# A written-out instruction order laid out anew, with GpSimd and SBUF-only VectorE work taking turns in the plan, and 150 warm-up matmuls of 256 columns in place of 50 of 512

## The chip, the cores and the metric

The kernel runs on one core of a Trainium2 chip. The metric is the device time of one execution in microseconds (us). Besides the 16 DMA engines the core has TensorE (PE; its weight loads are shown as PEld), VectorE (DVE), ScalarE (ACT), GpSimd (POOL) and SyncE (SP), which issues every DMA of this kernel. Each engine runs its own instructions strictly in the order in which the program lists them.

## The reference

Two stages. First a causal attention with a decay, for 8 batches, 8 heads, 576 positions and a head width of 64:

```python
scores = scale * q @ k.T
decay = cum[:, :, :, None] - cum[:, :, None, :]      # cum = cumsum(log(clip(f)))
scores = where(causal, -1e9, scores + decay); attn = softmax(scores)
attn_out = attn @ v
```

The heads' outputs side by side are `x` (8 x 576 x 512). The second stage is a mixture of four experts. Each expert is a causal attention of its own on `x` (`wq[e]`, `wk[e]`, `wv[e]` of 512 x 64), followed by `wo[e]`. A gate `x @ w_gate` picks two of the four experts for each position, and their outputs are added with softmax weights.

## The kernel before, in words

The work is cut into 48 units. A unit is a pair of heads of the first stage (named `a`, batch, pair: `a0_0` to `a7_3`) or a pair of experts of the second (`m0_0` to `m7_1`). Each unit goes through the same steps, each of them a Python generator that emits one or a few instructions between two `yield`s:

- `prep_attn` (lines 395 to 418) loads q and k as `xin`; ScalarE writes the rounded high parts into `kq` and `ka`, and VectorE subtracts them from the input to get the low parts (line 415, 64 x 1152). Two or three copies inside SBUF are DMAs. `prep_moe` (525) makes q and k of an expert pair by 96 matmuls `pp` (line 541) from `xh` and `xl`. `moe_front` (428) makes the values and the gate: matmuls `pv` (line 444), then a row of small VectorE operations.
- `max_pass` (563) computes scores without the decay's low part with matmuls (line 570) into two PSUM buffers `psm`; VectorE takes masked row maxima from them (lines 576, 591, 623, 630). PE turns the maxima (line 635), ScalarE negates them (638), and two small DMAs write them as a row of `kq` (issued at line 393).
- `scores` (660) computes the scores again, transposed, maxima included (lines 669 and 670, two PSUM buffers `pss`). ScalarE takes exp (686 to 725) into `P`, GpSimd zeroes what is above the diagonal (656, 689, 727) and adds the parts of `P` for the row sums into `R` (733 to 739).
- `attend` (745) multiplies by the values (line 758). For two units together `row_sums` (788) and `apply_rows` (839) sum, invert and scale (VectorE lines 811 to 829, 849, 876), and for experts `project_out` (880, matmuls at line 892) writes the output.

Every operation with two numbers has its line in the profile. VectorE operations whose operands all lie in SBUF are those of lines 415, 876, 814 to 829, 630 and most of those of the gate (470 to 502). GpSimd's masks and sums (656, 689, 727 to 739) lie in SBUF too.

Nothing but the string `ORDER` decides in which order the generators advance. Each two characters of it name one of 293 tasks (a step of a unit, or one of five tasks for constants, weights and warm-up), and each time a task is named, its generator runs to its next `yield`. The emitted instructions are then tied together in that order on every engine, SP included. `SLOTS` says for each buffer name which of its copies (two, three or six) the next tile takes. `4w` is `keep_warm` (line 214): matmuls of zeros by zeros into one PSUM bank that nothing reads. `4y`, `4x`, `4z` and `4A` are constants, the decay's rows, their spreading and the weights; `00`, `02`, `03`, `04` are `prep_attn`, `max_pass`, `scores` and `attend` of unit `a0_0`, `05` and `07` `prep_attn` and `max_pass` of `a0_1`.

The loop at line 951:

```python
    for x, y in zip(digits[::2], digits[1::2]):
        i = DIGITS.index(x) * len(DIGITS) + DIGITS.index(y)
        if i not in started:
            started[i] = iter(tasks[i]())
        next(started[i], None)
```

Of the kernel before, what the change touches and what calls it, by code (L numbers as in the profile page):

```python
# [32 lines left out]
0j0j0j080j0f0f08080o0o080f0j0f0j0f080f0j04030o0f0j0o0t0j080j0j0j0j0f0j090j08090f0q0q0q0j0f0f0f0f0f0f0f0q0f0q0q0q
0q0q0o0o0f0j0a0f0j0t090k0f0f0f0f0q0f0v0a0a0a0f0k0a0f0q0d0k0k0A0t0q0q0a0k090k0q0k0k0f0q0g0A0k0k0t0a0t0k0k0k0k0k0t
0a0t0i0q0q0v0q0q0k0v0v0v0k0k0k0a0F0k0k0v0v0q0q0k0q0k0k0v0v0k0g0f0q0k0f0k0k0p0g0q0b0b0q0A0b0b0b0q0b0v0v0v0l0v0q4w
0r0r0r0r0v0b0v0k0r4A4A0A0A0v0v0r0r0k0b0v0f0v0v0k0C0r0v0v0v0b0b0r0r0r0b0r0r0t0C0v0u0C0v0v0r0r0C0r0r0r0r0C0l0A0m0m
0r0r0r0b0r0r0m0C0w0F0w0w0l0m0m0F0b0m0M0C0C0m0m0m0s0v0A0n0B0n0w0w0w0w0w0C0n0n0C0C0C0C0C0H0n0w0n0M0w0w0w0w0n0n0n4A
# [48 lines left out]
2X2X2X30233030322O3131313131312T31313130312T2T2V2T2T2X2T2T2O2X2T31312X2X31352X2O3135311k352O31323525323532323232
# [36 lines left out]
434v4v4v4v4v4v4v  # L123
# [5 lines left out]
xin 01010101011010101001010101101010  # L129
# [16 lines left out]
NWARM = 50  # L146
# [4 lines left out]
def tile_decay_attention_moe(ctx: ExitStack, tc, qk, v, f, w_gate, wq, wk, wv, wo, out):  # L151
    nc = tc.nc
# [850 lines left out]
```

## Time and profile before

| | |
|---|---|
| time, median of 3 runs | 710.05 us (709.86 to 710.18) |
| the profiled execution's own time | 709.44 us |
| its span, first to last instruction | 707.7 us |
| mean granted TensorE clock | 0.990 |
| PE busy | 677.6 us, 96% of the span |
| VectorE, ScalarE, GpSimd busy | 582.2, 447.2, 444.9 us |
| bytes read from and written to HBM | 32.91 MB, 10.35 MB |

The profile shows one execution. A busy PE is not a PE at its best pace, since matmuls are pipelined and the profile models their ends: one matmul of 260 columns is shown with some 285 ns, while twelve in a row take about 1.45 us. The granted clock is told as a share of 2.4 GHz: 1.00 is 2.4 GHz and 0.50 is 1.2 GHz.

### The profile page before, as it was taken

How to read it: one execution, taken by the hardware profiler on the slowest of the kernel's cores; microseconds unless marked ns; L12 is line 12 of the kernel's file. 1: busy time of each engine (PE TensorE's matmuls, PEld its weight loads, DVE VectorE, ACT ScalarE, POOL GpSimd, SP SyncE). 2: the span in 40 equal slices, each digit the busy share in tenths (PEclk: the TensorE clock that was granted, in tenths of full speed). 3: DMA queues.
4: the chain of work that ended last, by engine and by line, in shares of the span. 5: the costliest groups of instructions: out<-in, count | busy, mean ns of one | idle time of the engine just before them, and what ended most of it. 6: DMA issues, size and time to landing. Idle time of an engine off the chain costs nothing.

```text
span 707.7 us, 15337 instructions
## 1 busy us (share of the span) xinstructions
PE 677.6 (96%) x5370; PEld 556.1 (79%) x5370; DVE 582.2 (82%) x1664; ACT 447.2 (63%) x961; POOL 444.9 (63%) x760
## 2 busy tenths in 40 slices
PE   8798999889999999999999999999999999999997
PEld 3675788668887898778887788788987788879874
DVE  6879988988899788979889888887889978775752
ACT  5676756566567756676586665667665755755544
POOL 7497486576676684676557653846945665653470
PEclk9699999999999999999999999999999999999999
DMA  5665432343173325442335233253333342222203
GB/s 169 171 161 158 107 105 68 88 115 81 36 189 119 88 57 161 112 142 66 87 82 175 74 118 97 59 140 113 83 97 101 107 136 55 51 79 53 50 16 119
DMA packets 31230, 72.23 MB, mean 102 GB/s; under 512 B 4137, under 2 KB 4617, under 8 KB 31153
## 3 DMA queue, kind: packets, MB, share of 16 engines
q1 hardware_dynamic: 31153, 71.25, 36.8%
q8 instruction: 42, 0.69, 0.4%
q14 instruction: 35, 0.29, 0.1%
HBM read 32.91 MB, written 10.35 MB: 61 GB/s over the span
## 4 chain that ended last, share of the span: by engine, by line
PE 71%; DVE 20%; ACT 3%; issue 3%; DMA 1%; POOL 0%; DVEq 0%; ACTq 0%
PE pp_m L541 12%; PE pv L444 7%; PE m_a L570 7%; PE s_a L669 6%; PE s_a L670 6%; PE ob_a L758 6%; PE po L892 5%; DVE ka_a L415 4%; PE ob_m L758 3%; DVE junk_a L576 3%; PE m_m L570 3%; PE s_m L669 2%; PE s_m L670 2%; PE oa_a L758 2%; PE warm L217 2%
## 5 line engine op out<-in xcount | busy, mean ns | idle before, releaser
L656 POOL TENSOR_SCALAR_AFFINE_SELECT P_a<-P_a 128x128 f32<-128x128 f32 x128 | 47.0, 372 | 104.5 <-ACT P_a L704 59.2
L669 PE MATMUL s_a<-ka_a 128*128 128x320 f32 (+4 forms) x384 | 108.4, 306 | 0.2 <-ACT pl L725 0.2
L570 PE MATMUL m_a<-kq 128*128 128x320 f32 (+4 forms) x384 | 95.0, 319 | 11.5 <-DVE mxs_a L576 8.3
L670 PE MATMUL s_a<-kq 128*128 128x320 f32 (+4 forms) x384 | 104.3, 298 | 1.1 <-DMA kq<-ms_a 1.1
L576 DVE CUSTOM_DVE_ANT_0 junk_a<-m_a,mask 128x448 bf16<-128x448 f32 (+2 forms) x192 | 91.7, 485 | 15.9 <-PE m_a L570 12.4
L570 PEld LDWEIGHTS m_a<-kq 128*128 128x128 f32 (+1 forms) x384 | 63.9, 185 | 25.9 <-DVE mxs_a L576 13.9
L669 PEld LDWEIGHTS s_a<-ka_a 128*128 128x128 f32 (+1 forms) x384 | 70.6, 184 | 6.8 <-issue 1.9
L549 ACT ACTIVATE kq<-pp_m 64x288 fp32r<-64x288 f32 x128 | 51.8, 405 | 37.7 <-PE pp_m L541 36.1
L733 POOL TENSOR_TENSOR R_a<-P_a 128x448 f32<-128x448 f32 x64 | 75.6, 1181 | 0.0
L554 DVE TENSOR_TENSOR ka_m<-pp_m,kq 64x288 fp32r<-64x288 f32 x128 | 58.2, 455 | 19.0 <-ACT kq L549 14.9
L670 PEld LDWEIGHTS s_a<-kq 128*128 128x128 f32 (+1 forms) x384 | 70.0, 184 | 2.6 <-DMA kq<-ms_a 1.7
L758 PE MATMUL ob_a<-P_a,va 128*64 128x320 f32 (+1 forms) x512 | 67.6, 406 | 0.0
L735 POOL TENSOR_TENSOR R_a<-R_a,P_a 128x320 f32<-128x320 f32 x64 | 61.0, 954 | 3.8
L686 ACT ACTIVATE P_a<-s_a 128x512 f32<-128x512 f32 x64 | 37.0, 595 | 29.0 <-PE s_a L670 28.5
L669 PE MATMUL s_m<-ka_m 128*128 128x192 f32 (+2 forms) x192 | 52.8, 300 | 2.0 <-ACT P_m L686 2.0
L758 PEld LDWEIGHTS ob_a<-P_a,va 128*64 128x64 f32 x512 | 35.8, 137 | 24.0
L670 PE MATMUL s_m<-kq 128*128 128x192 f32 (+2 forms) x192 | 51.3, 295 | 0.2 <-DMA kq<-ms_m 0.2
L415 DVE TENSOR_TENSOR ka_a<-xin_a,kq 64x1152 fp32r<-64x1152 f32 x32 | 48.7, 1521 | 1.1 <-ACT kq L403 0.3
L689 POOL TENSOR_SCALAR_AFFINE_SELECT P_a<-P_a 128x256 f32<-128x256 f32 x64 | 32.8, 518 | 26.0 <-ACT P_a L686 25.9
L576 DVE CUSTOM_DVE_ANT_0 junk_m<-m_m,mask 128x192 bf16<-128x192 f32 (+2 forms) x96 | 45.8, 485 | 3.2 <-PE m_m L570 2.2
L704 ACT ACTIVATE P_a<-s_a 128x448 f32<-128x448 f32 x64 | 34.1, 544 | 22.7 <-PE s_a L670 21.9
L656 POOL TENSOR_SCALAR_AFFINE_SELECT P_m<-P_m 128x128 f32<-128x128 f32 x64 | 20.3, 319 | 44.3 <-ACT P_m L704 26.7
(191 smaller groups left out, 2142.7 us busy)
## 6 DMA issues: line engine op xcount, KB each, us to landing
xin_a<-in_qk_dram SPq DMA_DIRECT2D x32, 576.0 KB
va<-in_v_dram SPq DMA_DIRECT2D x32, 320.0 KB
ka_a<-kq SPq DMA_DIRECT2D x32, 288.0 KB
ka_m<-kq SPq DMA_DIRECT2D x32, 288.0 KB
kq<-ka_a SPq DMA_DIRECT2D x30, 288.0 KB
out_dram<-outb SPq DMA_DIRECT2D x32, 256.0 KB
kq<-ex SPq DMA_DIRECT2D x47, 27.0 KB
kq<-ms_a SPq DMA_DIRECT2D x64, 2.5 KB
```

The lines of the kernel that those rows point to most:

```text
L415: nc.vector.tensor_tensor(lo, x[at], hi.bitcast(F32), ALU.subtract)
L541: nc.tensor.matmul(pp[:, :HS], w[:, c, es], x[c][:, gs], start=(n == 0), stop=(n == 3 * KC - 1))
L549: nc.scalar.activation(hv[h], src[h], AF.Copy)
L554: nc.vector.tensor_tensor(lo[:, h, gs], src[h], hv[h].bitcast(F32), ALU.subtract)
L570: nc.tensor.matmul(dst, qB[0:K, h, i0 : i0 + dst.shape[0]], kB[0:K, h, j0:j1], start=True, stop=True)
L576: nc.vector.tensor_tensor_reduce(jk[:, :n], src, mask[:, MW - n :], 1.0, init, ALU.add, ALU.max, acc)
L656: return nc.gpsimd.affine_select(pv, pv, [[1, 128]], ALU.is_ge, 0.0, base=0, channel_multiplier=-1)
L669: nc.tensor.matmul(dst, kaf[:, c : c + m], qA[:, h, i0:i1], start=True, stop=False)
L670: nc.tensor.matmul(dst, kqf[0:K, c + h * S : c + h * S + m], qB[0:K, h, i0:i1], start=False, stop=True)
L733: g.tensor_tensor(r[:, h, 128:S], q[:, 320:768], q[:, 768:1216], ALU.add)
L735: g.tensor_tensor(r[:, h, 256:S], r[:, h, 256:S], q[:, 1216:1536], ALU.add)
L758: mm = nc.tensor.matmul(dst[64 * h : 64 * h + 64, c0 : c0 + rhs.shape[-1]], vs[h][0:kp, blk], rhs, start=first, stop=last,)
```

## The change

`ORDER` is another list of the same steps. The generators are the same, and each of them runs through the same steps in its own sequence; only how they are interleaved differs. In the plan from which the new list was written, a VectorE operation on SBUF operands alone and a GpSimd operation never run at the same time. `SLOTS` differs in which copy a tile takes in ten of its rows (`P`, `xin`, `xh`, `mxs`, `psm`, `pss`, `ol`, `psx`, `xl`, `outb`, some of them in a few places only). `keep_warm` issues 150 matmuls of 256 columns, not 50 of 512.

Read step by step, the two lists begin so. Before, 43 warm matmuls stand ahead of the first matmul of `max_pass` of `a0_0`, and the other 7 right behind its first two. In the new list 94 stand ahead of it, and 56 stand in groups of 1 to 24 between the matmuls of the first three units, the last two of them just ahead of the second block of scores of `a0_1`. On VectorE, before, the two subtractions of `prep_attn` of `a0_1` stand behind the second and behind the last operation of `max_pass` of `a0_0`; in the new list both stand behind the last one. On GpSimd the small memset of `mxs` (line 566) with which `max_pass` of `a0_2` begins stands behind the first three masks of `a0_0` before, and ahead of the weights' last two parts and of all these masks in the new list. The last steps, from `attend` of `m7_1` on, have the same matmuls behind them in both.

```diff
 ORDER = """
-4y4y4y4y4y4y4y4y4y4y4y4y4y4w4w4x4x4x4x4x4w4w4w4w4w4w4w4w4w4w4w4w4w4w4w4w4w4w4w4w4w4w4w4w4w4w4y004y4A0000004x4w4w
-4w05054w4w4w4w4w4w4w4w4w4w05054w4w00004z024z4z0000024w4w4w4A4A4A4A4w4w4A4w4w4A4A024A024A050205020202020202024A0c
...
+4w4w4w4w4w4w4w4w4w4w4w4w4w4w4w4w4w4w4w4w4w4w4w4w4w4w4w4w4w4w4w4w4w4w4w4w4w4w4w4w4w4w4w4w4w4w4w4w4w4w4w4w4w4w4w4w
+4w4w4w4w4w4w4w4w4w4w4w4w4w4w4w4w4w4w4w4w4w4w4w4w4w4w4y4y4y4y4y4y4y4y4y4y4y4y4y4y4x4x4x4x4x4x4y000000004A050505
+00024A4A074w4w4w4w4w4w4w4w4w4w4w004w020500004z02024w4w020202024w4w4w4w4w4w020202024w4w4z020202020202024z4A024A4A
...
 SLOTS = """
-P 01010101101010101010101010101010101010101010101010
+P 01010101010101010101010101010101011010101010101010
...
-NWARM = 50
+NWARM = 150
 NACT = 2
...
     def keep_warm():
         wps = ptile(ps_o, "o", "warm")
         for _ in range(NWARM):
-            nc.tensor.matmul(wps, wz[:, 0:128], wz, start=True, stop=True)
+            nc.tensor.matmul(wps[:, :256], wz[:, 0:128], wz[:, :256], start=True, stop=True)
             yield
```

## Rows read from the trace of the kernel before

**Rows 1.** Busy time by stage: each engine's us and instructions, then clock, DMA share, GB/s.

```profile
12.50:36.00 23.50, 17.67 (x76) 13.40 (x73) 18.98 (x56) 15.13 (x24) 11.94 (x23) 0.71 0.73 188
36.00:100.00 64.00, 59.36 (x457) 45.51 (x456) 56.71 (x141) 42.32 (x87) 49.73 (x78) 1.00 0.48 133
100.00:680.00 580.00, 566.78 (x4645) 478.09 (x4645) 485.89 (x1427) 372.75 (x823) 365.34 (x626) 1.00 0.35 95
```

**Rows 2.** The same view, the stretches of 2 us around the lower clock.

```profile
16.00:18.00 2.00, 0.89 (x3) 0.48 (x3) 1.52 (x6) 0.47 (x1) 1.28 (x1) 1.00 0.82 269
...
20.00:22.00 2.00, 1.51 (x5) 1.09 (x5) 1.97 (x3) 0.27 (x1) 1.93 (x4) 0.50 0.76 219
...
32.00:34.00 2.00, 1.95 (x12) 1.74 (x11) 1.49 (x7) 1.31 (x4) 0.59 (x2) 0.73 0.52 159
```

**Rows 3.** PE in order of time: start, us, instructions, [idle before <- releaser].

```profile
1.26 11.67 PE L217 MATMUL warm<-wz 128*128 128x512 bf16 x43 [1.26 <-DVE wz L212]
12.58 0.61 PE L570 MATMUL m_a<-kq 128*128 128x192 f32 x2
13.03 1.69 PE L217 MATMUL warm<-wz 128*128 128x512 bf16 x7
...
16.73 0.59 PE L570 MATMUL m_a<-kq 128*128 128x256 f32 x2 [1.65 <-DVE mxs_a L576]
```

**Rows 4.** What VectorE waited for from 12.5 to 36 us: total us, times, longest.

```profile
DVE junk_a L576 <- PE m_a L570: 3.6, 5, 1.3
DVE junk_a L576 <- POOL mxs_a L566: 0.9, 1, 0.9
```

**Rows 5.** VectorE in order of time: its first maximum, and that of the third unit.

```profile
13.34 0.36 DVE L576 CUSTOM_DVE_ANT_0 junk_a<-m_a,mask 128x192 bf16<-128x192 f32 x1 [1.27 <-PE m_a L570]
...
32.38 0.36 DVE L576 CUSTOM_DVE_ANT_0 junk_a<-m_a,mask 128x192 bf16<-128x192 f32 x1 [0.93 <-POOL mxs_a L566]
```

**Rows 6.** GpSimd in order of time, around the memset that released it.

```profile
31.36 0.29 POOL L656 TENSOR_SCALAR_AFFINE_SELECT P_a<-P_a 128x128 f32<-128x128 f32 x1 [1.12 <-ACT P_a L704]
31.61 0.10 POOL L566 MEMSET mxs_a<- 64x2 f32 x1
```

**Rows 7.** The chain that ended last: start, us, what; runs without a wait, and a transfer.

```profile
75.57 2.79 DMA kq<-ms_a
...
163.14 1.45 PE pv L444 x12
...
301.68 1.40 PE po L892 x6
```

**Rows 8.** VectorE groups by shape: busy us, mean ns of one | idle before.

```profile
L415 DVE TENSOR_TENSOR ka_a<-xin_a,kq 64x1152 fp32r<-64x1152 f32 x32 | 48.7, 1521 | 1.1 <-ACT kq L403 0.3
L876 DVE TENSOR_TENSOR xl_a<-ot_a,xh_a 128x576 fp32r<-128x576 f32 x32 | 29.2, 914 | 4.4 <-ACT xh_a L868 4.0
```

**Rows 9.** Single lines of the kernel: min/median/max ns of one, first and last start.

```profile
L415 DVE TENSOR_TENSOR ka_a<-xin_a,kq x32: 1351/1354/2329, 9.3 to 584.4; 64x1152 fp32r<-64x1152 f32 x32
...
L876 DVE TENSOR_TENSOR xl_a<-ot_a,xh_a x32: 695/759/2983, 68.4 to 639.7; 128x576 fp32r<-128x576 f32 x32
...
L829 DVE STREAM_TRANSPOSE rr_a<-zt_a x16: 764/778/779, 59.7 to 628.6; 128x576 f32<-128x576 f32 x16
...
L737 POOL TENSOR_TENSOR R_a<-R_a,P_a x64: 585/599/1793, 38.2 to 622.9; 128x192 f32<-128x192 f32 x64
```

**Rows 10.** VectorE, then GpSimd, in order of time at 68.4 us: one collision.

```profile
68.41 2.98 DVE L876 TENSOR_TENSOR xl_a<-ot_a,xh_a 128x576 fp32r<-128x576 f32 x1 [1.24 <-ACT xh_a L868]
...
68.52 1.15 POOL L737 TENSOR_TENSOR R_a<-R_a,P_a 128x192 f32<-128x192 f32 x2
```

**Rows 11.** What PE waited for in the whole span: total us, times, longest.

```profile
PE mp_a L635 <- DVE mxs_a L576: 2.4, 5, 1.2
...
PE s_a L670 <- DMA kq<-ms_a: 1.1, 3, 0.5
PE mp_m L635 <- DVE mxs_m L576: 0.9, 3, 0.4
```

More of the change, by code (lines that the diff above doesn't have):

```diff
@@ L33 @@
[L33 to L37, printed above, removed]
@@ new lines @@
+034w0303030e030e0e0e0j070303030303030e0e03030e0303030h0h0e03030o0h0o0h08080e0e0e0e0e4w4w0808080e0h0e080e0h0e0e04
+0e0e080e0808030e0e0e0j080808080c0j0j034z4z08080j040806080j0j0j0808080e0j0j080j080j080o0e0j0j0f0f08080f0j0j0t080f
+0o0f0f0j0j0f0f0o04080j0j0h0j0j080j080f0o030908080d0t0q0j0f0j0j090j0q0q0f0f0f0f0q0q0q0q0f0f0f0q0f0f0f0f0f0f0f090k
+0q0k0a0v0o0q0k0t0k0o0k0p0k0t0t0a0f0k0a0q0k0i0a0q0q0a0t0a0q0f0f0f0k0k0q0k0k0k0k0A0k0q0a0a0a0t0k0q0g0g0q0k0q0q0q0k
+0k0q0v0t0k0k0k0k0k0k0q0q0q0v0v0F0f0k0g0C0f0A0A0b0b0b0b0v0k0k0q0b0q0f0v0v0v0F0v0k0b0l0v0v0v0v0r0r0v0A0v0r0r0v0A0v
@@ new lines @@
+0v0k0v0v0r0r0r0v0v0v0b0k0r0r0C4A0C0l0b0r0r0r0b0v0v0r0l0r0u4z0b0H0r0r0l0r0r0C0b0C0C0C0C0r0r0r0A0r0r0v0m0m0m0F0w0r
+0m0w0m0v0m0b0w0w0w0w0m0m0A0s0m0n0C4A0n0F0n0n0w0C4A0w0C0n0w0w0C0w0M0F0b0n0H0n0w0C4A0w0w0n0M0M4A4A0n0w0w0n0C0w0w0n
+0H0H0n0w0w0s0s0N0H0N0A0w0N0w0C0w0w0N0w0r0n0N0M0C0H0N0r0r0r0r0N0n0C0x0M0N0N0C0H0C0M0N0C0r0r0C0C0H0N0B0N0C0C0H0N0R
+0F0C0C0C0N0N0N0N0N0N0N0N0N0N0N0N0N0N0N0H0D4A0H0N0N0N0N0w0w0w0w0w0w0N0N0D0D0H0H0H0N0D0D0M0M0M0M0M0D0N0F0H0H0M0M0M
+0M0M0M0M0D0D0D0H0D0H0F0H0H0e0y0y0D0H0O0D0D0H0H0Y0D0O0O0D0R0R0D0D0D0D0H0D0O0R0H0+0H0D0D0D0D0y0y0y0y0y0y0D0R0O0D0D
@@ new lines @@
+0O0R0R0N0R0R0M0M0O0H0M0D0D0D0D0M0y0O0Y0I0O0I0M0I0M0M0M0M0O0M0z0O0z0O0I0O0O0M0M0M0O0z0I0I0I0I0I0I0M0M0M020G0z0O0x
+110R0x0O0O0M0R0M0R0M0M0O0O0z0I0I0I0I0I0I0I0R0R0O0O0O0a0R0R0R0R0R0R0I0I0I0Y0N0M0M0O0O0O0R0O0I0I0I0I0I0I0I0I0I0I0I
+0Z0S0R0z0z0R0R0R0R0R0R0R0R0Y0R0R4w0M0M0E0E0R0R0M0E0Y0Y0R0S0R0R0R0P0S0S0S0S0P0P0P0S0S0S0z0z0P0P0P0P0z0P0M0M0z0z0S
+0P0S0S0S0S0P0z0P110Y0J0J0P0S0S0S0S0S0J0S0P0P0P0P0P0P0P0P0P0P0P0P190P0P0S11110S0K0+0S0S0S0S0S0K0K0M0+0K0Q110Q0Q11
+0K0+0+0T0P0P0K0P110K0+0+0m0T0+0T0+0K0T0T0T0M0T0T180+0+0+110+0T0T0T0+0+1d0M0Y0M0K0T0d0T0T0T0+0+0+0T0+0T1313130P0+
@@ new lines @@
+0L0+0+0T130+0T0T0+0L0+0+0+0L0T0T000T130T0T0T130L0T1f0T0L0T18180T0T13130L0L0L0U0-0-13130L1313130-0-130-0L0-0L0-0-
+13131813130L120-0-0-13130-0-1313131d0V0V0V0V0-180-0-0L0-0-0-13131k1a130-0-130-1k1a1k1d0V0V0-1a1a1a1a1a0V0V1k1k1k
+1k140U1a1a1k181d1d1414141a1a0Z1a1a1a1l0-0-0-1k1k1k1k1k1k1k0V1d0U0-0-1414141k0-0-1d1a1a1a1k100V1k0W1a0W140-1a1a1a
+0W1414141414141k141k14141a101k10140W4w0W1k181k18141k1a1a1k141414141a14141k1f1f1k1k1l1k1k1l1l1l1l1l1f1f1f1f1f1f1l
+1m0W0W1l1l141l1a1a1b1b1b1l1l1l1l1l1f1f1f1f1l1l1f1l1b1b1l1f1f0W1b1414141b14141d1l1b1b0W0W1b181b1f1l1b1l1l0W1f1l1f
@@ new lines @@
+1f1f0W0W1k1k1k1k0W1l151l4A4A161f16161f1b1b1b1b151b1b1b1b1f151l1p1l1f1b1b1b1b1b1b1b1b1b0W1l1l1l1l1l16161616161y1w
+1f1p4A1p161f1l1m1l1k1m1m1m1m1p1p1p1p1p1p1p1p1p1p1m1m1g1g1g1g1g1g1p171e1m171m1p1p1m1m1p1p1g1g1g1g1w1p1p1p1m0W1p1p
+1p1m174A174A1k1p1m1k170W1m1p1p1g1g1m1g051g1m1m1p1p1p1p171p171p1b1p1g1g1m4z1k1k1m1g17171g1g1g1g1g1g1k1l1p1m1p1m0L
+1l1c1w1w1w1c1c1w1m1m1m1k1m1k1g1g1g1g1g1g1h1w1q1q1q1p1q151q1n1q1n1k1b1n1n0X1q1q1q1n1B1n1h1h1n1n1n1n1B1q1q1g1g1q1q
+0X0X1n1q1q1n1n1q1n1p0X1q1q1q1q1i1i1q1n1n1i1n1q1i1w1i1n1i1i1y1I1n1n1n1n1n1q1q1y1y1n1n1i1D0X1q1q1q0X1B0O171k1i1B1y
@@ new lines @@
+1y1y1y171B1o1y1y0X1r171r1n1B1B1n1r1j1r1y1y1y1r1r1j1j1j1r1n1r1D1r1r1j1y0X1r0X1N1y1D1D1y1r1r061n1n1y1r1r1r1y1y1y1r
+1r1y0X1r0B1y1j1j1r1r1r1r1r1B1r1k1o1y1y1y1o1r1r1k1r0X171D0X1y1y0X0X1r1r1r1I1D1D1D0X1D1s1D1z1I1n1D1D1D1j1z1z1z1D1j
+1z1D1z1z1j1D1z1j1D1D1z1D1D1z1z1s1D1z1k1k1k1D1t1t1z1z1z1I1I1z1j1D1z1z1z1s1t1t1t1D1t1m1z1z1j1D1U1N1U1U1z1z1z1K1I1K
+1U1K1K1U1U1I1U1z1D1U1C1z1z1D1U1K1K1z1K1U1U1U1U1U1U1U1V1x1N1K1U1E1U1U1U1E1E1K1K1K1K1K1K1E1U1U1U1E1J1E1E1U1N041K1U
+1U1U1E1N1N1E1E1E1t1E1E1K1U1N1P0u1U1P1P1K1K1K1K1A1E1A1t1t1t1U1z1A1z1E1E1K1V1E1V1K0y1E1K1N1u1u1E1K1K1E0E1E1E1E1E1I
@@ new lines @@
+1z1W1V1V1V1P1P1K1P1P1P1P1V1V1V1V1V1V1V1V1V1V1K1P1P1P1P1L1V1V1V1V1V1V1P1V1U1u1E1u1V1V1E1E1E1E1E1E1V1V1P1P1L1L1L1P
+1P1U1U1U1U1U1U1L1P1U1U1F1G1G1G1P1P1P1u1u1L0y1u1L1U1L1u1u1L1V1G1G1G1G1L1V1P1P1P240M0U1u1u1P1V1G1L1P1L1L1L1A1L1L1V
+1Z1L1L1V1u1u1V1V1V1V1V1L1L1L1W1W1G1W1L1L1u1W1W1Z1Z1H1Q1Q1Q1L1Q1Z1Q1Q1H1H1H1Z4y2g1L1F1Z1Z1W1Q1W1W1Z1Z1Z1Z1u1D1Z1Z
+1Q1Q1H1H1u1Q1Q1L1Q1Q1Q1O1Z1W1W1W1L1Z1Z1L1L1Z1Z1Z1Z1W1Z1W1F1W1x1Q1V1W1Z1Z1Z1Z1Z1Z1Z1Z1Z1Z1Z1Z1L1W1Q1Q1Q1Q1Q1Q1Q1Q
+1Q1Q1W0X1+1W1W1W1W1W1+24241M1u1M1+241W241U1M1W1W1W1R1+0a241Z1U1+1v1U241Z1+1+1+1+26291Z1R1Q1Q1Q1Q1Q1Q1X1X1X1v1v1Z
@@ new lines @@
+1+1+1X1+1+1Z1+1X1X1X1X1U1+1+1v1H1L1H111H1H1X1X241+291+1X1H1X1X1H1U1+1+1U1+1+1X1S1S1S1+1X1X1X1X1X1+1S1S1+1X261+1+
+1X1S2926261v1v261X1X1X1X1S1S1R1v1v1v1S1v2626262b262929291-1-1-1-1-1-26261v1v261X261-1X1X261X1H1X1-1-1T2626261u26
+1-1Y26262629291-1-1-1-261-1-1-1-261Y1Y0K1v2b1v1-2b1-2b261-1T2l2h26262b1-1-1-1-1-1-1-1-261T2b1T1v1T1T1T1v1v2b2b2b
+202g2g2b271T2b2b1v2b270S1T2b2i2l1-1-2b1v272b1v1T1T1T2b27271X272b272b2g2g1U1U1U201T212121270F21212121272a27272727
+27272s2b2b2b212i2s272727271v272i27272b2i2b2b212s242i2b2127272s2b2i2i2i2s272727272i2s2s2s1v272s2i2l2s0J2i2b2s1616
@@ new lines @@
+2s2s2i2i2i2i2s222c2c2l2l2i2s272s2i222n2c2i2c2c2c2i2i2i2i2s2s2s2s2s072i2i2i252s2s2s0p202c252c2c2l2s2t0A2i2c2n2n2n
+2n2n2n2c2c2c222s2s2s222g2n2n2g2c2c2i2c2c270v222l2s2c2c2c2c2c2c2c2c2c282g2c2c2c2c2c2h2s132j2t2m0z2t2j2n2n2n221T22
+2n222j2j2t2t2t2t2t2t282t2t2t2n2s2s220G2t2t2s2s2s2s2j282n2n2j2j2t2t2t2t2t2j222j222x2n2E2n2d2F2n2e2e2s2e2s2s2e2j2j
+2j2d2d222j2j2j2n2n2j2j2t2t2e2e2e2t2t222n2n2j2t2e2j2n2t2t2t2t2t2e2l2n2j2j2u2t2t2t2t2t2x2t2n2j2n262E2t2x2x2x4A2x2j
+2t2x2u1J2u2u2u2u2x0j2x0q2x2u2o2x2j2j2o2o2u2o2x2x2o2o2f2x2u2x2j2j2f2j2j2j2x2o2o2u2o2x2x2u2o2u2o2u2t1Y2u2x2x2x2x2f
@@ L130 @@
[L130 removed]
+xin 01010101010110101011010001001010
 ka 012012012012012012012012012012012012012012012012
[L132 to L133 removed]
+xh 01234501234035124043512043512043512043512
@@ L143 @@
 yl 0101010101010101
-outb 010101010101010101000000010
+outb 010101010101010101010101010
 """
-NWARM = 50
+NWARM = 150
 NACT = 2
```

153 lines of the change are left out of this document (56 added, 97 removed).

## The prediction

> **What bounds the kernel now.** I read the busy time by stage first [rows 1]. Between 100 and 680 us PE is busy for 566.78 of 580 us, so over four fifths of the span PE sets the pace and has only 13.2 us of shown idle time to give. Between 36 and 100 us it has 4.6 us (64.00 less 59.36), and VectorE is busy for 56.71 of 64, 89%. Between 12.5 and 36 us it is different: PE is busy for 17.67 of 23.5 us at a mean granted clock of 0.71, and VectorE for 18.98. The reader is to see three stages with three answers. At the start VectorE's row of maxima sets the time, and PE, at half its clock, makes VectorE wait. In the middle stage VectorE is close to full. After that PE is.
>
> Next I read the start in steps of 2 us [rows 2]. From 16 to 18 us PE is busy for 0.89 of 2 us with the clock still at 1.00; from 20 to 22 us the clock is 0.50, that is 1.2 GHz; between 32 and 34 us it comes back (mean 0.73). What went before the fall is in PE's own order of time [rows 3]: 43 warm matmuls fill PE from 1.26 us, seven more end at about 14.7 us, and then PE waits, 1.65 us ahead of one matmul alone. So warm matmuls held the clock up, and it fell some microseconds after they were used up.
>
> Last I read who made VectorE wait [rows 4]: 3.6 us for PE in five waits, the first of them 1.27 us ahead of its very first maximum [rows 5], and 0.9 us for a memset on GpSimd. The two together are the 4.5 us that VectorE has idle in this stage, so nothing else holds it up there.
>
> **The change part by part: the warm matmuls ahead of the first real one.** Before, 43 x 512 = 22,016 columns stand there, in the new list 94 x 256 = 24,064, 2,048 more. Six matmuls of 512 columns take 1.40 us in a row without a wait, twelve of 260 take 1.45 us [rows 7]: 0.456 and 0.465 ns a column. So 2,048 columns are 0.93 us. Two of 260 columns cost 9 ns more than one of 512, of which 4 ns are columns, so 47 pairs add 0.24 us. That makes 1.2 us. Low end 0.9; high end 2.1, with the added columns at the half clock. The first matmul of the maxima began at 12.58 us behind the last but one of the 43 [rows 3], so PE was held by them, not by data, and the whole 1.2 us reaches VectorE. **+1.2 us.**
>
> **The other 56.** They are 14,336 columns or 6.7 us at that pace, where seven took 1.6 us before: 5 us more on PE's in-order queue. They cost nothing if PE would have stood idle: it has 5.8 us idle between 12.5 and 36 us [rows 1]. A mean clock of 0.71 over 23.5 us means 13.6 us at half clock. At PE's busy share of 0.75 that is about 10 us of work that takes 5 at the full clock, so there is room for about 11 us. The largest group, 24 or 2.8 us, stands ahead of the turning of `a0_0`'s maxima (line 635), for which VectorE has about 1.3 us left to do. That turning comes up to 1.5 us late, but the first scores stand behind the maxima of `a0_1`, and these wait for VectorE's two subtractions, 2 x 1.35 us [rows 9], which now stand together. Without that cover it costs 1.5 us. **0.**
>
> **The clock at the start.** With PE's gaps filled I expect 2.4 GHz to stay. VectorE's four later waits for PE sum to 2.3 us. They are waits for one or two matmuls that run at half clock, so I take three quarters, 1.73 us, not all. The memset of the third unit's maxima ran at 31.61 us right behind a mask that had waited 1.12 us for ScalarE [rows 6], and VectorE waited 0.93 us for what follows it [rows 5]. In the new list it stands ahead of all masks, and I take the 0.93 us whole. Together **-2.7 us**. Bounds: -3.2 (every wait gone) and 0 (the clock falls all the same and PE is as late). ScalarE cannot hold back more than this: 15.13 us busy of 23.5 [rows 1].
>
> **SP's queue.** The new list moves two fills of the decay's rows and the values' load of `a0_0` ahead of the second of the two small DMAs with the maxima of `a0_1`. These issues stand one behind the other on SP, so that row lands later by about the time of two issues. Its readers, the scores of `a0_1`, stand behind a whole block of `a0_0`'s scores, so I cost it at nothing. If they did wait, the nearest row is a transfer of such maxima that the chain shows with 2.79 us [rows 7].
>
> **The turns.** On the chip the two engines take turns already. At 68.41 us a subtraction (line 876) took 2.98 us while two of GpSimd's additions ran [rows 10]; the median of that line is 759 ns and its mean 914 [rows 8, 9], so 32 of them lose 5.0 us. The subtractions of line 415 lose 32 x (1521 - 1354) ns = 5.3 us, and GpSimd's additions of line 737 have a median of 599 ns and a longest of 1793. No list takes these collisions away by itself; a plan that knows of them can leave PE other work meanwhile. I counted that in both lists, with the matmuls between two steps priced at the pace above. Of the 48 turnings of maxima, 13 had less than 0.5 us of PE work between VectorE's last step and themselves, in the new list 5. PE waited 3.3 us for these [rows 11], 1.2 of them in one wait at the start. 8 of 13 of the other 2.1 us are -1.3 us. Against it, 18 first blocks of scores, not 13, stand within 1 us of PE work behind the issue of their maxima's DMA; PE waited 1.1 us for these DMAs [rows 11], and 5 of 13 more are +0.4 us. **-0.9 us** in all. Bounds: -17.8 us (all of PE's idle time from 36 to 680 us) and, as no row of before limits what a new list adds, PE's idle time from 100 to 680 us once more, +13.2 us.
>
> A rule speaks against the turns. Transposes of 576 columns inside SBUF (line 829) show 764, 778 and 779 ns as least, median and longest over 16 [rows 9]: no collision ever, though the plan makes them take turns too. The Trainium skill, "SBUF — State Buffer", section "Who interferes with whom", says that a VectorE instruction contends with GpSimd if it has two SBUF inputs (against GpSimd's reads) or runs in a two-port mode, and not otherwise; the subtractions and the transposes of this trace agree with it. By that rule the plan keeps GpSimd waiting for nothing behind transposes, and by the rows above it does so for 24 x 0.78 = 18.7 us, hidden as long as GpSimd is idle a third of the time (365 of 580 us busy, [rows 1]). That is a rival below.
>
> **Sum.** 709.44 (the profiled execution: a span of 707.7 and 1.74 around it) + 1.2 - 2.7 - 0.9 = 707.0 us. The median of the three runs shown is 0.6 above the profiled execution, so I predict 707.6 us.
>
> **The rivals.**
> - *The start gives nothing.* Zeros in pieces of 256 columns between waits do not hold the clock, or VectorE's waits have another cause. For it: 23.5 us hold only 4.5 us of VectorE's waits. Against it: the 43 in a row held it. The head's 1.2 us stay: 709.44 + 1.2 - 0.9 + 0.6 = 710.3, no change. Chance 0.18.
> - *The turns pay.* If half of PE's 17.8 us goes, the time is 709.4 - 1.5 - 8.9 + 0.6 = 699.6; a quarter gives 704. For it: VectorE is 89% busy in the second stage, where collisions hurt most. Against it: PE's named waits for VectorE after the start are small [rows 11]. Chance 0.15.
> - *Slower: PE's queue stands behind the maxima's DMA.* Five more first blocks of scores stand close behind it, and PE does nothing past a waiting matmul. One such transfer took 2.79 us in the chain [rows 7]; five are 14 us. Two of the five in full (5.6 us) outweigh the 2.4 us won and reach 709.44 + 3.2 + 0.6 = 713.2; one alone nearly does. For it: DMA takes its time whatever the plan says of VectorE. Against: leads of other steps grew. Chance 0.17.
> - *Slower: turns planned too widely.* If a third of the 18.7 us reaches PE through later row sums, +6.2 - 1.5 gives 714.7. Against it: in the list only 1 of 24 row sums stands within 1 us of PE work behind GpSimd's last addition, 3 before. Chance 0.08.
>
> **How the numbers follow.** The forecast has 0.42, with a range of its own from 706.8 (every wait gone, the low end of the head) to 709.0 (half of the waits gone). Two lists that differ in thousands of places can differ by waits that no row shows, so the range takes in the quarter and more of PE's idle time at the low end and the DMA's two to three waits at the high end: 701.5 to 714. About a tenth lies below and a tenth above. This kernel's measurement can tell about 0.2%, 1.4 us. Faster than 708.6: the turns' 0.15 and most of the forecast, 0.36, together 0.51. Within: 0.06 of the forecast and 0.17 of the first rival, 0.23. Slower: 0.26.
>
> **What would show it.** Right: a clock of 1.00 from 8 to 40 us, the first matmul of line 570 at about 13.8 us, VectorE's first maximum of the third unit (32.38 us, [rows 5]) at about 30.9, PE's idle time from 100 to 680 us near 12 us. The start's step is wrong if the clock shows 0.50 again or VectorE still waits 3 us for PE there. The turns' step is wrong if PE's waits for VectorE grow, or if waits for the maxima's DMA appear with several microseconds; then the time ends above 711.

## The result, and the profile after

The changed kernel takes 703.93 us (median of 4 runs, 703.83 to 704.04) against 710.12 us before (4 runs, 709.86 to 710.60): a ratio of 0.9912 [0.9895, 0.9929], 6.2 us less. The range of 701.5 to 714 held it and the sign was right. It lies below the forecast's own range of 706.8 to 709.0, by 2.9 us, and the single time forecast, 707.6 us, was 3.7 us too high. The profiled execution took 704.02 us with a span of 702.3, 5.4 us less than before. Every line number of the code below `SLOTS` is one higher than before.

Busy time by stage, the columns as in [rows 1]:

```profile
12.50:36.00 23.50, 21.26 (x149) 16.01 (x148) 19.83 (x57) 15.52 (x24) 13.77 (x25) 1.00 0.76 197
36.00:100.00 64.00, 58.59 (x463) 46.38 (x458) 55.19 (x145) 42.75 (x88) 52.80 (x80) 1.00 0.49 134
100.00:680.00 580.00, 567.48 (x4669) 479.29 (x4669) 484.27 (x1431) 375.59 (x828) 374.67 (x629) 1.00 0.35 95
```

The clock of the first stage is 1.00 in place of 0.71. In the two others PE's busy time, which I had taken as the measure of what can be won, hardly moves: 58.59 for 59.36 us, and 567.48 for 566.78. What moves is the count beside it, of the matmuls that run in a stretch. From 36 to 680 us the two rows count 463 + 4669 = 5132 where they counted 457 + 4645 = 5102 [rows 1] (a matmul that runs across an edge counts on both sides of it). Thirty more, at the 122 ns that one takes on the mean (566.78 us / 4645), are 3.7 us of work done earlier.

PE in order of time, from its first warm matmul (columns as in [rows 3]):

```profile
1.26 12.69 PE L218 MATMUL warm<-wz 128*128 128x256 bf16 x94 [1.26 <-DVE wz L213]
13.71 0.50 PE L571 MATMUL m_a<-kq 128*128 128x192 f32 x2
...
18.69 2.79 PE L218 MATMUL warm<-wz 128*128 128x256 bf16 x24
21.32 0.27 PE L636 MATMUL mp_a<-ident,mxs_a 128*10 128x128 f32 x1
```

The first matmul of the maxima begins at 13.71 us, 1.13 later than before [rows 3]. The group of 24 warm matmuls holds the queue until 21.3 us; the turning stands right behind it. VectorE meanwhile does the two subtractions that now stand together:

```profile
19.93 1.41 DVE L416 TENSOR_TENSOR ka_a<-xin_a,kq 64x1152 fp32r<-64x1152 f32 x1
21.37 1.35 DVE L416 TENSOR_TENSOR ka_a<-xin_a,ka_a 64x1152 fp32r<-64x1152 f32 x1
```

VectorE in order of time, its first maximum and that of the third unit, and then its waits from 12.5 to 36 us:

```profile
14.36 0.36 DVE L577 CUSTOM_DVE_ANT_0 junk_a<-m_a,mask 128x192 bf16<-128x192 f32 x1 [2.30 <-POOL low L273]
...
31.29 0.36 DVE L577 CUSTOM_DVE_ANT_0 junk_a<-m_a,mask 128x192 bf16<-128x192 f32 x1
```

```profile
DVE junk_a L577 <- POOL low L273: 2.3, 1, 2.3
DVE junk_a L577 <- PE m_a L571: 1.4, 3, 0.5
```

VectorE starts 1.02 us later than before and is 1.09 us ahead of before at the third unit [rows 5], so it makes up 2.1 us between. The wait for the memset is gone, and the waits for PE behind the first maximum are 1.4 us where they were 2.3 [rows 4, 5]. The wait of 2.3 us is the one ahead of the first maximum. It is put down to a constant on GpSimd; PE's first two matmuls, at 13.71 us, come last there.

The operations that collide, by line: least, median and longest ns (to be read against [rows 9]), then the first of them as a group, with its mean (to be read against [rows 8]):

```profile
L416 DVE TENSOR_TENSOR ka_a<-xin_a,kq x32: 1351/1355/2510, 9.3 to 575.6; 64x1152 fp32r<-64x1152 f32 x32
...
L877 DVE TENSOR_TENSOR xl_a<-ot_a,xh_a x32: 729/758/2103, 67.8 to 635.0; 128x576 fp32r<-128x576 f32 x32
...
L738 POOL TENSOR_TENSOR R_a<-R_a,P_a x64: 584/597/1790, 35.4 to 616.2; 128x192 f32<-128x192 f32 x64
```

```profile
L416 DVE TENSOR_TENSOR ka_a<-xin_a,kq 64x1152 fp32r<-64x1152 f32 x32 | 49.9, 1561 | 1.2 <-ACT kq L404 0.3
```

The collisions are still there. The mean of the first subtraction rose from 1521 to 1561 ns, the other's fell from 914 to 902, and GpSimd's addition still has a longest of 1790 ns. VectorE's busy time fell from 582.2 to 575.9 us all the same, in its small operations (the 16 of line 814, 128x18, have 418 ns on the mean before and 199 after), and GpSimd's rose from 444.9 to 454.4: part of the loss changed sides.

### The profile page after: what moved, and what is told of

The parts are those of the page before. It is cut to its first block, busy times and chain, and to the rows that moved or that the text cites. A ratio compares the mean times of both kernels' runs of the same rounds, so it can differ in the third digit from the quotient of the medians.

```text
span 702.3 us, 15565 instructions
## 1 busy us (share of the span) xinstructions
PE 675.6 (96%) x5470; PEld 562.1 (80%) x5470; DVE 575.9 (82%) x1664; ACT 448.3 (64%) x961; POOL 454.4 (65%) x760
## 4 chain that ended last, share of the span: by engine, by line
PE 68%; DVE 18%; ACT 4%; issue 4%; DMA 3%; POOL 2%; SPq 0%; DVEq 0%; ACTq 0%; POOLq 0%
PE pp_m L542 12%; PE pv L445 7%; PE m_a L571 6%; PE po L893 6%; DVE ka_a L416 6%; PE s_a L670 5%; PE s_a L671 5%; PE ob_a L759 5%; PE ob_m L759 4%; PE m_m L571 4%; DVE junk_a L577 3%; PE s_m L670 3%; PE s_m L671 3%; PE oa_a L759 2%; PE sm_a L798 2%
## 5 line engine op out<-in xcount | busy, mean ns | idle before, releaser
L670 PE MATMUL s_a<-ka_a 128*128 128x320 f32 (+4 forms) x384 | 106.3, 301 | 1.1 <-DMA ka_a<-kq 0.6
L657 POOL TENSOR_SCALAR_AFFINE_SELECT P_a<-P_a 128x128 f32<-128x128 f32 x128 | 49.4, 391 | 84.9 <-ACT P_a L705 42.3
L571 PE MATMUL m_a<-kq 128*128 128x320 f32 (+4 forms) x384 | 92.0, 312 | 9.0 <-DVE mxs_a L577 6.6
L571 PEld LDWEIGHTS m_a<-kq 128*128 128x128 f32 (+1 forms) x384 | 61.8, 181 | 22.7 <-DVE mxs_a L577 12.3
L736 POOL TENSOR_TENSOR R_a<-R_a,P_a 128x320 f32<-128x320 f32 x64 | 64.5, 1008 | 3.7
L738 POOL TENSOR_TENSOR R_a<-R_a,P_a 128x192 f32<-128x192 f32 x64 | 48.7, 763 | 4.0
L416 DVE TENSOR_TENSOR ka_a<-xin_a,kq 64x1152 fp32r<-64x1152 f32 x32 | 49.9, 1561 | 1.2 <-ACT kq L404 0.3
L416 DVE TENSOR_TENSOR ka_a<-xin_a,ka_a 64x1152 fp32r<-64x1152 f32 x32 | 49.0, 1532 | 0.9
```

What stands on the lines that cost most here:

```text
L416: nc.vector.tensor_tensor(lo, x[at], hi.bitcast(F32), ALU.subtract)
L571: nc.tensor.matmul(dst, qB[0:K, h, i0 : i0 + dst.shape[0]], kB[0:K, h, j0:j1], start=True, stop=True)
L657: return nc.gpsimd.affine_select(pv, pv, [[1, 128]], ALU.is_ge, 0.0, base=0, channel_multiplier=-1)
L670: nc.tensor.matmul(dst, kaf[:, c : c + m], qA[:, h, i0:i1], start=True, stop=False)
L736: g.tensor_tensor(r[:, h, 256:S], r[:, h, 256:S], q[:, 1216:1536], ALU.add)
```

## The experiments

The experiments ran on three chips, and each kernel is compared with the kernel before on the same chip. Runs there spread over 1 to 5.5 us, more than those shown so far. Where a kernel joins parts of the two lists, `SLOTS` is laid out for its own order.

### The start alone, and the start left out

The list is cut behind 264 steps, at about 46 us, where the two orders differ in two steps only. The first kernel takes the new list up to there, with its 150 warm matmuls, and the old one behind it; the second the reverse.

```diff
 ORDER = """        # first kernel; the second swaps + and -
-4y4y4y4y4y4y4y4y4y4y4y4y4y4w4w4x4x4x4x4x4w4w4w4w4w4w4w4w4w4w4w4w4w4w4w4w4w4w4w4w4w4w4w4w4w4w4y004y4A0000004x4w4w
+4w4w4w4w4w4w4w4w4w4w4w4w4w4w4w4w4w4w4w4w4w4w4w4w4w4w4w4w4w4w4w4w4w4w4w4w4w4w4w4w4w4w4w4w4w4w4w4w4w4w4w4w4w4w4w4w
...
-NWARM = 50
+NWARM = 150
```

> The new list up to the point ahead of the values of a0_1 (about 45 us; the first 264 steps apart from the warm matmuls, which both lists have in common up to one), with all 150 warm matmuls, then the old list. Theory A (the start gives what was forecast, 1.4 us, and the new order after it gives the other 4.5): 708.3 to 709.0. Rival B (all of it comes from the start, and the lists are equal after it): 703.7 to 704.5. A third, C (the two parts help only together): 710.

> The reverse: the old list with its 50 warm matmuls of 512 columns up to the same point, then the new list. Theory A: 705.2 to 706.2, with the clock at 0.50 between 19 and 33 us as before. Rival B: 709.7 to 710.5. C: 710.

New start, old rest: 709.63 us (10 runs, 707.41 to 711.18), 0.9989 [0.9975, 1.0003] of the 710.38 before. Old start, new rest: 708.90 us (10 runs, 705.80 to 709.82), 0.9975 [0.9960, 0.9990]. The start is worth 0.75 us and can't be told from nothing; I had forecast 1.5, and this kernel lies above the range that theory A gave it. The rest without the start is worth 1.5, which lies between the theories, and the two add up to 2.2 of 6.2. What is lost shows in the second kernel: a piece of the chain that ended last, then ScalarE and PE in order of time, then PE alone in a stretch of 2 us (us, busy time and instructions, clock, DMA share, GB/s):

```profile
47.73 4.38 DMA xin_a<-in_qk_dram
```

```profile
52.13 1.16 ACT L403 ACTIVATE kq<-xin_a 64x1152 fp32r<-64x1152 f32 x1 [4.22 <-DMA xin_a<-in_qk_dram]
...
54.06 0.53 PE L570 MATMUL m_a<-kq 128*128 128x192 f32 x2 [2.16 <-ACT ms_a L638]
```

```profile
56.00:58.00 2.00, 2.00 (x15) 0.50 0.50 107
```

The old start issues this load of q and k at 47.7 us, as the kernel before does (47.3); the new list issues it at 43.3. Its reader on ScalarE stands at the new list's place and waits 4.2 us, PE waits 2.16 us behind it, and then the clock falls. So this seam costs about two microseconds that neither whole list has, and the second number is too small for the rest of the order.

### The warm matmuls alone

In the new list only the 94 at the head are kept; and the old list gets all 150, each ahead of the same real matmul as in the new one.

```diff
-NWARM = 150        # new list
+NWARM = 94
```

```diff
-NWARM = 50         # old list; in ORDER 4w stands 150 times, placed as in the new list
+NWARM = 150
...
-            nc.tensor.matmul(wps, wz[:, 0:128], wz, start=True, stop=True)
+            nc.tensor.matmul(wps[:, :256], wz[:, 0:128], wz[:, :256], start=True, stop=True)
```

> The new list with the 94 warm matmuls ahead of the first real one, without the 56 that stand between the first units' matmuls. If the 56 hold the clock: it falls to 0.50 at about 20 us, VectorE waits 1 to 2 us more for PE before 36 us, and the time is 705.0 to 706.5. If the clock played no part in the gain: 703.4 to 704.4.

> The old list with the 150 matmuls of 256 columns, each ahead of the same real matmul as in the new list. If the clock's gain stands by itself: the clock stays at 1.00, the first maxima come 1.2 us later, VectorE's waits for PE shrink by 1.7 us, and the time is 709.2 to 709.9 (the 0.9 us of waiting for the memset stays). If the warm matmuls only stand in the way: 711 to 712.

New list without the later 56: 706.46 us (7 runs, 703.59 to 707.94), 0.9948 [0.9929, 0.9967]. Old list with all 150: 711.85 us (10 runs, 710.64 to 713.13), 1.0028 [1.0018, 1.0038]. Busy time from 12.5 to 36 us, and VectorE's wait, of the first kernel and then of the second:

```profile
12.50:36.00 23.50, 16.42 (x78) 12.90 (x76) 17.98 (x51) 13.20 (x22) 9.42 (x20) 0.71 0.70 176
```

```profile
DVE junk_a L577 <- PE m_a L571: 5.7, 5, 2.9
```

```profile
12.50:36.00 23.50, 20.14 (x127) 14.60 (x125) 17.19 (x51) 13.09 (x22) 11.47 (x21) 0.93 0.65 164
```

```profile
DVE junk_a L577 <- PE m_a L571: 6.1, 4, 2.8
```

Without the 56 the clock is back at a mean of 0.71, the value of before. VectorE waits 5.7 us for PE; 2.9 of them stand ahead of its first maximum, as 2.3 do in the new kernel, and behind it there are 2.8 where the new kernel has 1.4. So those 56 hold the clock. What that is worth can be read by the ratios to the kernel before, since the new kernel ran on other chips: 0.9948 less 0.9914 (the new kernel run again, below) is 2.4 us, with intervals that touch.

The old list with all 150 is 1.5 us slower, as forecast for warm matmuls that stand in the way, but its clock did not stay at 0.71: it is 0.93 on the mean, and falls just where the group of 24 runs. PE in order of time, VectorE's wait behind that group, and the busy time around it:

```profile
20.73 4.37 PE L218 MATMUL warm<-wz 128*128 128x256 bf16 x24
```

```profile
25.60 0.36 DVE L577 CUSTOM_DVE_ANT_0 junk_a<-m_a,mask 128x192 bf16<-128x192 f32 x1 [2.36 <-PE m_a L571]
```

```profile
20.00:24.00 4.00, 3.88 (x20) 2.69 (x20) 3.14 (x9) 0.00 (x0) 1.45 (x4) 0.57 0.65 175
```

One of VectorE's two subtractions stands among the maxima of `a0_0` here, so PE waits 1.51 us at 16.7 us, the group comes 2 us later and takes 4.37 us, not 2.79, and VectorE has only one subtraction left to do meanwhile. The wait of 2.36 us shows that the group is not covered in this list. It is not a measure of the 1.5 us priced for that case. VectorE's first maximum comes at 14.83 us, 1.49 later than before, and that of the third unit at 34.34, 1.96 later [rows 5], so most of the delay in this execution is that of the longer head.

### What the collisions cost either list

GpSimd's four additions for the row sums are replaced by memsets of the same `R`, in the old list and in the new one. A memset writes `R` and reads nothing; the row sums are left out, so these two kernels do not compute the reference's result. The new kernel ran beside them.

```diff
-            g.tensor_tensor(r[:, h, 128:S], q[:, 320:768], q[:, 768:1216], ALU.add)
+            g.memset(r, 300.0)
...
-            g.tensor_tensor(r[:, h, 256:S], r[:, h, 256:S], q[:, 1216:1536], ALU.add)
+            g.memset(r[:, :, 128:S], 300.0)
...
-            g.tensor_tensor(r[:, h, 384:S], r[:, h, 384:S], q[:, 0:192], ALU.add)
+            g.memset(r[:, h], 300.0)
...
-        u["summed"] = g.tensor_tensor(r[0:64, :, 512:S], r[0:64, :, 512:S], p4[:64], ALU.add)
+        u["summed"] = g.memset(r[0:64, 0], 300.0)
```

> The new kernel once more, beside the others on this chip, where single executions of the kernel before lie between 708.5 and 712.0 us. If its gain of 6.2 us is the lists' own: a median of 703.5 to 705. If it hangs on where the clock's short falls (3.4 us each) happen to come: a spread from 703 to 708 and a median near 705.5.

> The kernel before with GpSimd's four kinds of additions for the row sums replaced by memsets of R of about the same length, which write SBUF and read nothing there (so the row sums are left out, and the output is not the reference's). If it is GpSimd's reads that VectorE collides with, the longest subtraction of line 415 falls from 2.6 us to 1.9 or less (the masks still read), and if these collisions cost time at the end: 704 to 707. If other work hides them: 709 to 710.5.

> The new kernel with the same replacement (the row sums are left out). If the new list wins by putting up better with collisions, it gains less than the old one: 702 to 703.5, and the distance between the two kernels shrinks from 6 to about 3 us. If its gain has nothing to do with collisions: the distance stays at 5.5 to 6.5 us.

The new kernel again: 704.33 us (4 runs, 703.70 to 705.54), 0.9914 [0.9899, 0.9929] of 710.72. Old list with memsets: 694.53 us (694.06 to 695.07), 0.9775 [0.9760, 0.9789]. New list with memsets: 691.38 us (690.39 to 692.24), 0.9734 [0.9718, 0.9750]. In the old list with memsets the subtractions show these ns, and the engines this busy time from 100 to 680 us:

```profile
L415 DVE TENSOR_TENSOR ka_a<-xin_a,kq x32: 1347/1353/1512, 9.3 to 569.6; 64x1152 fp32r<-64x1152 f32 x32
...
L876 DVE TENSOR_TENSOR xl_a<-ot_a,xh_a x32: 693/758/884, 67.3 to 624.8; 128x576 fp32r<-128x576 f32 x32
```

```profile
100.00:680.00 580.00, 573.78 (x4754) 484.43 (x4752) 468.52 (x1450) 377.58 (x834) 341.07 (x631) 1.00 0.35 95
```

The longest subtraction of line 876 fell from 2983 ns [rows 9] to 884 at the same median, and that of line 415 from 2329 to 1512 (in its second form from 2643 to 1532), below the 1.9 us expected. The times fell much further than expected: 694.53 us, not 704 to 707, and 691.38, not 702 to 703.5. The Trainium skill, "SBUF — State Buffer", section "Who interferes with whom", says that a VectorE instruction with two SBUF inputs contends with a GpSimd instruction that reads SBUF and not with one that only writes it. These rows agree.

The whole of the old list's loss to these reads is 710.72 - 694.53 = 16.2 us, more than the 13.2 us that PE showed idle between 100 and 680. The new list loses 704.33 - 691.38 = 12.95 us to them. So the lists stand 6.4 us apart with the reads and 3.15 without them, as expected for a list that puts up better with collisions: half of the gain, 3.2 us, goes away with the reads. In the half that stays is the start's share, 0.75 us by the run above. Two things are mixed in. A memset doesn't read `P`, so `P` also comes free earlier in both kernels; and the memsets are a little shorter than the additions (the first 1057 ns on the mean, its addition 1147 at the median). No run takes these apart from the collisions.

### Where in the span the order pays

Both lists are cut behind 872 steps, at about 130 us, where they differ in eight steps. One kernel takes the new list up to the cut and then the old, the other the reverse.

```diff
 0I0I0I0z0E0R0O0z0Y0Y11020O0O0R0R0R0z0M0R0R0M0M0M0R0R0O0O0O0R0R0O0R0R0R0S0R0z0z0R0R0R0R0R0S0S0S0S0S0E0Y0J0S0S0S0J
-0J0Y0P0P0P0P0P0P0S0S0S0S0S0z0K0K0z0P0S0P0S0Y0S0P0P0P0P0P0S0S0+0P0+0+0P0S0P0P0P0S0P180P0P0P0P0S0S0P0+0K0S0+0S0K0+
...
```

(The diff is of the second kernel against the one before: from the line taken out to the end of `ORDER`, the new list's steps stand.)

> The new list up to 130 us (872 steps, which both lists have in common up to seven), then the old one. If the stretch from 46 to 130 us brings what the start does not: 704 to 705.5. If the gain is spread over the whole rest: 707 to 708.5.

> The old list up to 130 us, then the new one. If the new order after 130 us is worth the 4 us between the new kernel and the new list up to 130 us by itself: 706 to 707. If it is worth that only behind the new start: 709 to 710.5.

New up to 130 us: 708.42 us (10 runs, 705.94 to 711.40), 0.9971 [0.9955, 0.9987] of 710.72. New from 130 us on: 706.12 us (5 runs, 705.47 to 708.82), 0.9937 [0.9916, 0.9958] of 710.95. Both lie where they were expected if the gain is spread, and the two add up within the spread: 2.3 + 4.8 = 7.1 us against 6.4 for the whole change. The order behind 130 us alone, with nothing of the start, is worth 4.8 us.

One step of this can be followed near 143 us. First the kernel before, VectorE, GpSimd, ScalarE and PE in order of time, then its busy time; then that of the kernel that is new from 130 us on:

```profile
142.18 2.23 DVE L415 TENSOR_TENSOR ka_a<-xin_a,kq 64x1152 fp32r<-64x1152 f32 x1
144.44 0.78 DVE L829 STREAM_TRANSPOSE rr_a<-zt_a 128x576 f32<-128x576 f32 x1
...
142.06 1.14 POOL L733 TENSOR_TENSOR R_m<-P_m 128x448 f32<-128x448 f32 x1
...
145.25 0.68 ACT L831 ACTIVATE rt_a<-rr_a 128x576 fp32r<-128x576 f32 x1 [3.55 <-DVE rr_a L829]
145.84 1.07 ACT L686 ACTIVATE P_m<-s_m 128x512 f32<-128x512 f32 x2
...
146.47 0.39 PE L669 MATMUL s_m<-ka_m 128*128 128x256 f32 x1 [2.04 <-ACT P_m L686]
```

```profile
143.00:147.00 4.00, 1.96 (x14) 1.65 (x13) 3.90 (x4) 1.66 (x3) 0.67 (x4) 1.00 0.58 130
```

```profile
143.00:147.00 4.00, 3.84 (x52) 3.01 (x51) 4.00 (x18) 3.06 (x7) 3.72 (x8) 1.00 0.97 286
```

The subtraction starts 0.12 us behind GpSimd's addition and takes 2.23 us instead of its median of 1354 ns [rows 9]. The transpose behind it on VectorE comes late, ScalarE waits 3.55 us for the transpose, and the exp that frees a bank of scores stands behind ScalarE's copy. PE's wait carries the name of that exp, not of VectorE or GpSimd. In the other kernel PE is busy for 3.84 of the same 4 us. Its count of 52 matmuls against 14 makes the step look larger than it is, since 32 of them are the gate's small ones, of 5 columns, which the kernel before runs later. PE in order of time, the kernel that is new from 130 us on and then the one before, the gate's matmuls and the first row sums of experts:

```profile
143.16 0.43 PE L509 MATMUL pg<-gt,ident 128*32 128x5 f32 x32
...
156.23 1.18 PE L797 MATMUL sm_m<-R_m,ones_col 128*32 128x288 f32 x16
```

```profile
158.29 0.43 PE L509 MATMUL pg<-gt,ident 128*32 128x5 f32 x32
...
158.87 1.18 PE L797 MATMUL sm_m<-R_m,ones_col 128*32 128x288 f32 x16
```

The row sums begin 2.6 us earlier. Of that, the two executions were already 1.0 us apart at 127 us, where both still run the same list (`attend`, line 758, at 127.26 and 128.26). By these two executions, then, about 1.6 us of the 4.8 come from this place. The collision did not vanish there; GpSimd has the worse of it and PE has other work:

```profile
139.19 1.35 DVE L415 TENSOR_TENSOR ka_a<-xin_a,kq 64x1152 fp32r<-64x1152 f32 x1
...
139.20 2.07 POOL L735 TENSOR_TENSOR R_m<-R_m,P_m 128x320 f32<-128x320 f32 x1
```

The subtraction takes its usual time, and the addition, which starts 0.01 us behind it, takes 2.07 us; the kernel before shows 0.87 for this shape at 140.56 us, where no subtraction runs. (The whole new kernel has a pause of its own at 140 us; it stands in the last section.)

### A shorter head: a version that might beat both

The new list with 80 warm matmuls at its head, and once more with 12 instead of 24 in the large group.

```diff
-NWARM = 150        # 14 fewer 4w at the head of ORDER
+NWARM = 136
...
-NWARM = 136        # second kernel: 12 fewer in the group ahead of the turning as well
+NWARM = 124
```

> The new list with 80 warm matmuls, not 94, ahead of the first real matmul (136 in all). In the profiles so far that matmul starts between 11.9 and 14.3 us, the later the later the clock comes up. If PE is held there by the warm matmuls alone and VectorE sets the pace up to 36 us: it starts 1.5 us earlier and the time falls from 704.3 to 702.5 to 703.3. If data or the second stage hold it back: 704 to 705.

> The same with the group of 24 warm matmuls ahead of the turning of a0_0's maxima cut to 12 (124 in all). If VectorE's two subtractions cover that group, as forecast: the same time as with 80 at the head, within 0.4 us. If the maxima of a0_0 are late through it: another 0.5 to 1.3 us less. If the shorter group lets the clock fall: 1 to 2 us more.

With 80: 704.57 us (4 runs, 703.91 to 705.39), 0.9914 [0.9891, 0.9936] of 710.95. With 12 in the group as well: 705.03 us (703.05 to 707.07), 0.9916 [0.9889, 0.9944]. Neither beats the new kernel's 0.9914, and the gain expected of the shorter head (702.5 to 703.3 us) did not come. The second spreads over 4 us, too much to tell 0.4. PE's first real matmul of the first:

```profile
11.86 0.50 PE L571 MATMUL m_a<-kq 128*128 128x192 f32 x2
```

It begins 1.85 us earlier than in the new kernel, and the end does not move. In this execution the second subtraction of `a0_1` collides (2.38 us at 19.46 us), and VectorE's first maximum of the third unit, at 30.48 us, is only 0.8 us earlier than in the new kernel. A lead at the start is worth little at the end here, which fits the start's 0.75 us above.

## Why the prediction was right, and which term was too small

The range held the time because it had been widened on both sides for waits that no row shows. The sum behind it had the start about right and the turns far too small, and that the time lay inside owes more to the width than to the sum.

**The head, +1.2 us: right.** 1.13 us measured at the first real matmul. The shorter head shows that such a delay hardly reaches the end.

**The other 56, 0: right as far as the runs show.** The turning in the new list came 1.4 us after VectorE's last maximum of `a0_0`, near the 1.5 forecast, VectorE had its two subtractions to do until 22.7 us, and half the group gave no better time. Without the cover, in the old list, VectorE waited 2.36 us behind the group; the price of 1.5 us for that case was not measured by itself.

**The clock, -2.7 us: right in kind.** The clock is 1.00 from 12.5 to 36 us, and falls back to a mean of 0.71 when the 56 are taken out. The memset's wait is gone whole. VectorE's gain is 2.1 us by the third unit, against 2.7 forecast. PE's first `attend` shows the sum of head and clock: it begins at 35.14 us, before at 36.52, 1.4 us earlier where 1.5 was forecast. At the end of the kernel the start was worth less, 0.75 us by its own run.

```profile
35.14 0.87 PE L759 MATMUL oa_a<-P_a,va 128*64 128x256 f32 x8
```

**SP's queue, 0, and the rival of the maxima's DMA: it didn't come.** PE's longest wait of that kind is half a microsecond, in this row of its waits from 36 to 680 us, which stands under those for VectorE's maxima; the second fence has the same waits for VectorE before:

```profile
PE m_a L571 <- DVE mxs_a L577: 6.4, 7, 1.9
PE mp_a L636 <- DVE mxs_a L577: 2.6, 3, 1.7
...
PE s_m L671 <- DMA kq<-ms_m: 1.0, 2, 0.5
```

```profile
PE m_a L570 <- DVE mxs_a L576: 4.8, 6, 1.2
...
PE mp_a L635 <- DVE mxs_a L576: 1.2, 4, 0.5
```

**The turns, -0.9 us: this is the term that was mis-sized.** It measured about 4: the span is 5.4 us shorter and 1.4 of them stand at 35 us; by itself the order behind 130 us gave 4.8. The sum had been made from the waits that carry the name of the maxima's turnings. These waits did not fall: behind the start they rose from 1.2 to 2.6 us for `mp_a`, and those of the maxima's own matmuls from 4.8 to 6.4. The prediction had named just this, growing waits of PE for VectorE, as the sign that the turns' step is wrong, with a time above 711 us. The sign came, and the time was 704. So the step that failed is the one that took PE's named waits for what the order can win.

PE's idle time was a poor measure as well. I expected 12 us between 100 and 680; it is 12.5, before 13.2, and from 36 to 680 us it is 17.9 in both. By that view nothing was won, while 24 more matmuls were begun from 100 to 680 us. The ends of matmuls are modelled, so short delays between them can be shown as busy time. One wait that went is that near 143 us: a collision caused it two engines further on, and in PE's list it had ScalarE's name. For the rest of the 4 us no wait that went is shown.

The rival "the turns pay" put 704 us on a quarter of PE's idle time. Its number came true and its reason did not, since that idle time did not fall. I gave it 0.15 because PE's named waits for VectorE are small. That argument failed: the name at the end of a chain need not be the one at its beginning.

**The rule against the turns.** The chip doesn't keep the plan's turns: collisions stay. The rival of turns planned too widely (714.7 us) had the plan holding GpSimd back, and GpSimd's additions became a wait of PE only once, of 0.2 us.

**What stays open.** Half of the whole gain goes away with the reads of the row sums. That it is bound to the collisions, and not to the earlier release of `P`, is argued and not shown. For the rest that is not the start's, about 2.4 us, no single cause was found. No run separates `ORDER` from `SLOTS` either.

## What to carry to other kernels

To size what collisions on SBUF cost, replace the reads of one side by memsets and time that, and ask what else the memsets set free: here 16 us of 710 went, more than PE showed as idle between 100 and 680 us. Compare how many instructions of the bounding engine two traces begin between the same marks, not only how long it is busy; over a short stretch take the start of one and the same step instead, since a matmul of 5 columns counts like one of 512. Warm-up matmuls in the gaps of an in-order engine cost nothing only as long as the next real one behind them would have waited anyway; look for what makes it wait before adding them.

## What the runs showed of the hardware that was not expected

The moment from which matmuls run at full pace differs from execution to execution, though all begin with the same zeros at 1.26 us. PE alone in steps of 1 us (us, PE's busy time and instructions, clock, DMA share, GB/s), the changed kernel:

```profile
4.50:5.50 1.00, 1.00 (x6) 1.00 1.03 401
5.50:6.50 1.00, 1.00 (x9) 1.00 1.03 419
6.50:7.50 1.00, 1.00 (x12) 1.00 0.33 134
```

The count doubles at about 6 us, and at about 5 in the kernel with 80 at the head. It has those that run across an edge on both sides; begun are four or five matmuls of 256 columns a microsecond, and nine later. The granted clock is written as 1.00 throughout: the count shows the half pace, the column doesn't. With 94 at the head, in the executions profiled, the first real matmul began between 13.27 and 14.29 us.

Second, the clock can fall late in the span, behind a pause of PE. The changed kernel, PE in order of time and then PE alone in steps of 2 us; then the same kernel in another execution (the run beside the memsets):

```profile
142.01 0.61 PE L571 MATMUL m_a<-kq 128*128 128x256 f32 x2 [1.85 <-DVE mxs_a L577]
```

```profile
142.00:144.00 2.00, 1.99 (x7) 0.61 0.97 265
144.00:146.00 2.00, 2.00 (x10) 0.53 0.66 130
```

```profile
142.00:144.00 2.00, 0.65 (x4) 1.00 1.01 206
144.00:146.00 2.00, 1.93 (x12) 1.00 0.98 278
```

In the first execution PE waits 1.85 us for VectorE's maxima and then runs at half clock until 145.9 us. In the second it is idle for 1.35 us of the stretch from 142 to 144, and the clock stays at 1.00; there it falls at 60 us instead (0.50 from 60 to 62). The kernel that is new behind 46 us shows such a fall behind its pause at 52 us (above), and the kernel before, with its pause of 2.04 us at 144.4, shows none. So a pause of 2 us may cost as much again in clock (an estimate: 3.9 us at half clock do 2 us less work), and a trace without the fall doesn't say that there won't be one. That these falls make part of the spread of the runs is an inference; no run here tests it.
